# Batch 1's split rows: q's two halves in one product over two PSUM banks, their sums on VectorE at once, the squares' sum on GpSimd

## The chip, the cores and the metric

The kernel runs on one core of one Trainium2 chip. The metric is the device time of that core in microseconds, as the median of several runs. The engines are TensorE (PE; its weight loads are shown apart as PEld), VectorE (DVE), ScalarE (ACT), GpSimd (POOL) and SyncE (SP), which issues most transfers. Each works through its own queue in order and waits on semaphores for the others.

## What is computed

An attention over channels, for two batches of 6016 tokens and 256 channels, followed by a gated layer and a second layer:

```python
def _attn_ref(q, k, v, tau) -> np.ndarray:
    qn = q / (np.linalg.norm(q, axis=1, keepdims=True) + 1e-06)
    kn = k / (np.linalg.norm(k, axis=1, keepdims=True) + 1e-06)
    s = kn.transpose(0, 2, 1) @ qn / tau
    s = s - s.max(-1, keepdims=True)
    a = np.exp(s)
    a /= a.sum(-1, keepdims=True) + 1e-09
    return (v @ a).astype(np.float32)
...
    gate = 1.0 / (1.0 + np.exp(-(x @ w_gate)))
    val = x @ w_val
    return (gate * val @ w_out).astype(np.float32)
...
    h = x @ w_in
    g = h - np.tanh(h)
    return (g @ w_out).astype(np.float32)
```

The scores of a batch are a 256 x 256 matrix, a sum over all its tokens, so no token of batch 1 can go through the layers before all of batch 1's q and k have been multiplied. The layers have 1536 and 2048 hidden channels.

## The kernel before

**Arithmetic.** A float32 value is held as two rounded halves, hi and lo, and a product is made of three: hi with hi, lo with hi, hi with lo. `split` makes the halves: ScalarE copies with rounding (L104), VectorE subtracts (L105).

**Units.** The main loop goes over units. A unit of layer 1 is 512 tokens and 128 hidden channels: 6 products into a gate tile and 6 into a value tile (`ps`, lines L475, L476, L480 of the helpers `prod_h` and `prod_l`), the sigmoid (L515, ScalarE), gate times value (L516, VectorE). A unit of layer 2 is 6 products into one tile `h`, then `s2_a`: on ScalarE two functions of `h` (L539, L540) and two of the result `u` (L541, L543), on VectorE L544 and L546, which read `h`, then L547 and L548. L546 is the last reader of `h`, and it overwrites `u` in place, so it also stands behind ScalarE's L541 and L543. `part_b` splits a unit's result (L575 ScalarE, L576 VectorE) and `part_c` multiplies it, three units later, into the output tiles `y` or `o`. The units of both layers are sorted by a position number, and so stand mixed.

**PSUM.** There are eight banks of 512 float32 columns. Four belong to the accumulators, and four are a ring (`ring`, tag "ring", `bufs=4`): every gate, value and `h` tile and every side product takes a bank of it. A new tile waits on TensorE for the last reader of the tile that had its bank.

**The side work.** From the third token tile on, batch 1's q and k are multiplied beside the layers. The token rows r = 0 to 46 hold 128 tokens each; r = 0 to 3 were multiplied earlier and are only squared here, and r = 4 to 46, 43 rows, are the split rows. A list `side` holds the steps, some of which follow each unit, spread evenly. A split row has three: `side_split` (halves of q and k into `hl`), `side_square` (ScalarE squares the raw row in place, L666), `side_mm`. The last first calls `side_sum`: VectorE adds the squares to `nacc` (L673), and the loads of row r + 2 are issued on SP, which wait for that add. Then `qk_products` (L283 to L285) makes six products of 256 columns into one ring bank. `side_add`, VectorE's add of that bank to the score sum `sacc` (L686), is not issued there but one unit later, ahead of that unit's side steps, through the list `after`. When all rows are done, `nacc` is summed over the partitions by TensorE (`side_norm_mm`).

Of the kernel before, what the change touches and what calls it, by code (L numbers as in the profile page):

```python
# [18 lines left out]
B, S, D = 2, 6016, 256  # L19
# [50 lines left out]
def attn_moe_kernel(  # L70
# [12 lines left out]
    nc = tc.nc  # L83
    ctx.enter_context(tc.manual_schedule())
    mm = nc.tensor.matmul
# [10 lines left out]
    def ring(name):  # L96
        return pp.tile([P, CH], F32, tag="ring", bufs=4, name=name)
# [5 lines left out]
    def split(hi, lo, src, eng=nc.vector):  # L103
        nc.scalar.copy(hi, src)  # L104
        eng.tensor_sub(lo, src, hi.bitcast(F32))  # L105
# [66 lines left out]
    def pump(n):  # L172
        for _ in range(n):
            if stream[0] is not None and next(stream[0], 1) == 1:
                stream[0] = None
# [64 lines left out]
    def fill(g):  # L240

        if g == 0:
            S1.append(bank("o1", "S1"))
        ps = S1[0].rearrange("p (c j) -> p c j", c=2)
        for r in range(filled[0], filled[0] + FILL[g]):
            for c in range(2):
                mm(ps[:, c], fq["k", r][:, c * P : (c + 1) * P], fq["q", r], start=r == 0 and c == 0, stop=r == sum(FILL) - 1, skip_group_check=True)
        filled[0] += FILL[g]
# [28 lines left out]
                w = qk0["k", r0][:, r, c * P : (c + 1) * P]  # L277
                mm(S0[c], w, qk0["q", r0][:, r, :], start=r0 + r == 0, stop=r0 + r == R - 1)  # L278

    def qk_products(ps, qh, ql, kh, kl, first, last):  # L280
        for c in range(2):
            cs = slice(c * P, (c + 1) * P)
            mm(ps[:, c], kh[:, cs], qh, start=first and c == 0, stop=False, skip_group_check=True)  # L283
            mm(ps[:, c], kh[:, cs], ql, start=False, stop=False, skip_group_check=True)
            mm(ps[:, c], kl[:, cs], qh, start=False, stop=last, skip_group_check=True)  # L285

    def refine(rn, s0, n2):
        nc.vector.tensor_mul(rn, rn, n2)
# [70 lines left out]
    def spill():  # L359
        f = full.pop(0)  # L360
        nc.sync.dma_start(wgv_d[f], wgv_t[f].bitcast(F32))
# [66 lines left out]
    ps = ring("spread")  # L428
# [25 lines left out]
    for ic in range(2):  # L454
        cs = slice(ic * P, (ic + 1) * P)
# [63 lines left out]
    def s2_mm(i, m):  # L519
        n = tiles[i][3]  # L520
        h = yhl[i]
        need(f"wi{m // 2}")
        ps = ring(f"h{i}_{m}")
        prod(ps, n, [pair(wi_t[m // 2], (m % 2) * 2 * P + j * P) for j in range(2)], [(h[:, 0, j, :n], h[:, 1, j, :n]) for j in range(2)])
        live[2, i, m] = ps
# [35 lines left out]
    def part_a(u, between=lambda: None):  # L561

        if u[1:] not in live:
            (s1_mm if u[1] == 1 else s2_mm)(*u[2:])
        between()
        (s1_a if u[1] == 1 else s2_a)(*u[2:])
# [42 lines left out]
    def part_c(u):  # L609
        _, kind, i, c = u  # L610
        _, _, pos, n = tiles[i]
        hl = live.pop((kind, i, c))
        last = (K1 if kind == 1 else K2) - 1
        need(f"wo{c // 2}" if kind == 1 else f"wv{c // 2}")
        acc, wt, tag = (yps, wo_t, "y") if kind == 1 else (ops, wv_t, "o")
        if c == 0:
            acc[i] = [bank(f"{tag}{o}", f"{tag}{i}_{o}") for o in range(2)]
        ws = [pair(wt[c // 2], (c % 2) * D + o * P) for o in range(2)]
        if u[1:] == LAST:
            return finish(hl, ws, pos)  # L620
        x = [(hl[:, 0, :n], hl[:, 1, :n])]
        skip = kind == 2 and i == NT - 1
        for o in range(2):
            prod_h(acc[i][o], n, [ws[o]], x, c == 0, skip)
        for o in range(2):
            prod_l(acc[i][o], n, [ws[o]], x, c == last, skip)
        if c == last:
            if kind == 1:
                pool = mp if i % 2 == 0 or (yp is None and i > NYQ) else yq[0] if yp is None else yp
                h = pool.tile([P, 2, 2, NM], F32R, tag="yhl", name=f"yhl{i}")  # L630
                for o in range(2):
                    split(h[:, 0, o, :n], h[:, 1, o, :n], yps[i][o][:, :n])
                yhl[i] = h
            else:
                for o in range(2):
                    t = m2.tile([P, NM], F32, tag="out", bufs=2, name=f"out{i}_{o}")
                    nc.scalar.copy(t[:, :n], ops[i][o][:, :n])
                    nc.sync.dma_start(outT[o * P : (o + 1) * P, pos : pos + n], t[:, :n])


    qp, qctx, q2ctx, q1 = None, ExitStack(), ExitStack(), {}
# [10 lines left out]
    def side_load(r):  # L652
        if r < R:
            raw = qp.tile([P, 2, D], F32, tag="raw", bufs=2, name=f"raw1_{r}")
            for t, src in ((0, q), (1, k)):
                nc.sync.dma_start(raw[:, t, :], token_rows(src, 1)[:, r, :])
            q1["raw", r] = raw

    def side_split(r):
        raw = q1["raw", r]  # L660
        hl = qp.tile([P, 2, 2, D], F32R, tag="hl", name=f"hl1_{r}")
        split(hl[:, 0], hl[:, 1], raw)
        q1["hl", r] = hl

    def side_square(r):
# [2 lines left out]
    def side_sum(r):  # L668
        raw = q1.pop(("raw", r))
        if r == 0:  # L670
            nc.vector.tensor_copy(q1["N"], raw)
        else:
            nc.vector.tensor_add(q1["N"], q1["N"], raw)  # L673
        side_load(r + 2)

    def side_mm(r):
        side_sum(r)
        hl = q1.pop(("hl", r))
        ps = ring(f"qk1_{r}").rearrange("p (c j) -> p c j", c=2)
        qk_products(ps, hl[:, 0, 0, :], hl[:, 1, 0, :], hl[:, 0, 1, :], hl[:, 1, 1, :], True, True)  # L680
        q1["ps", r] = ps
        after.append(r)

    def side_add(r):
        ps = q1.pop(("ps", r))
        nc.vector.tensor_add(q1["S"], q1["S"], ps)  # L686

    def side_norm_mm():
        ps, ones = ring("norm1"), q1["ones"]
# [76 lines left out]
            units.append((max(pos, START2 + DENSE * (i * K2 + m)), 2, i, m))  # L766
    units.sort()
    nside, started, side0 = len(side), 0, None
    qb, qc, after, awq = [], [], [], []

    ahead = [(1, t, K1 - 1) for t in (0, 1, NT - 1)] + [(2, t, K2 - 1) for t in (0, 1, NT - 2)]
    m2 = None
# [1 line left out]
    def step_b():  # L774
        u = qb.pop(0)
        part_b(u)
        qc.append(u)
# [4 lines left out]
    def aw0(f):  # L782
        need(f"wgv{f}_0", f"wgv{f}_1")
        for ic in range(2):
            aw_block(aT0, rs[0], wgv_t[f], ic, aws[0][f], f"aw0_{f}_{ic}")
        pump(2 + sum(owed))
        owed.clear()
# [20 lines left out]
    for u in units:  # L808
        at, kind, i, c = u
        if kind == 1 and i == 0 and c % 2 == 0 and c // 2 + 1 < NW // 2:  # L810
            if c // 2 + 1 < len(FILL):
                fill(c // 2 + 1)
            aw0(c // 2 + 1)
        if kind == 1 and i == 0 and c >= SPILL and full:
            spill()
        if kind == 1 and i == 1 and c == 2:
            t = cst.tile([P, NM], F32, name="s1_out")
            nc.vector.tensor_copy(t, S1[0])
            nc.sync.dma_start(s1_d, t)
        if kind == 2 and c == 0:  # L820
            while i not in yhl:
                if qb:
                    step_b()
                part_c(qc.pop(0))
        if kind == 2 and i == 0 and c == 0:
            pump(1000)
            cctx.close()
            m2 = ctx.enter_context(tc.tile_pool(name="m2", bufs=1, reuse_waits="tile"))
        if qb and len(qc) == LAG - 1 and qc[0][1:] in ahead:
            part_a(u, lambda: part_c(qc.pop(0)))  # L830
        else:
            part_a(u)
        if qb:
            step_b()
        qb.append(u)
        if u[1:] == (2, NT - 1, K2 - 2):
            s2_mm(NT - 1, K2 - 1)
        while len(qb) + len(qc) > LAG:
            part_c(qc.pop(0))
        if kind == 1 and i == 0 and c % 2 and c // 2 + 2 < NW // 2:  # L840
            owed.append(PUMP0)
        else:
            pump(PUMP0 if i == 0 else PUMP1)
        if kind == 1 and i == 0 and c == K1 - 1:
            pump(1000 if cst is None else 0)
        if cst is None and c + 2 >= NW - 2 and stream[0] is None:
            open_w2()
        if kind == 2 and i == NYQ and c == K2 - 1:
            yctx.close()
            side0 = at  # L850
        if side0 is not None:
            if after:
                side_add(after.pop())
            want = min(nside, int((at - side0) * nside / (SIDE_END - side0)) + 1)
            while started < want:
                if side[started] is not None:
                    side[started]()
                started += 1
        if awq:
            side_aw(*awq.pop(0))  # L860
        if kind == 1 and i == TPB - 1 and c % 2 == 1:
            awq += [(c // 2, 0), (c // 2, 1)]
# [46 lines left out]
```

## Time and profile before

| | us |
|---|---|
| median of 3 runs (lowest, highest) | 2305.57 (2305.44, 2306.1) |
| the profiled execution's own time | 2305.91 |
| its span, first to last instruction | 2303.8 |
| TensorE busy | 2297.8 (100%), 10434 products |
| VectorE busy | 1818.0 (79%), 2896 instructions |
| ScalarE busy | 1580.8 (69%), 2884 instructions |
| GpSimd busy | 74.6 (3%), 57 instructions |

TensorE's products are pipelined: one of 512 columns is shown as 0.39 us long, and the next starts 0.23 us after it, so starts are to be read, not lengths. The time of the engines is the union of their instructions. The chain that ended last is the work that set the end, followed back from the last instruction.

### The profile page before, as it was taken

The numbers are of one execution on the slowest core, as the hardware profiler recorded it, in microseconds if no ns is written. First come the engines' busy times: TensorE is split into PE (matmuls) and PEld (weight loads), VectorE is DVE, ScalarE is ACT, GpSimd is POOL, SyncE is SP. The second block draws the span as 40 slices with busy tenths as digits, with TensorE's granted clock in tenths as the row PEclk, the third lists the DMA queues.
The fourth block names the chain that finished last, engine by engine and source line by source line (L and its number), as shares of the span: only waits on it lengthen the run. The fifth ranks groups of instructions, "written<-read, shape, count | busy, mean of one in ns | idle before, by whom it ended". The sixth has DMA issues, their size and how long they took to land.

```text
span 2303.8 us, 28351 instructions
## 1 busy us (share of the span) xinstructions
PE 2297.8 (100%) x10434; PEld 1928.6 (84%) x10434; DVE 1818.0 (79%) x2896; ACT 1580.8 (69%) x2884; POOL 74.6 (3%) x57
## 2 busy tenths in 40 slices
PE   9999999999999999999999999999999999999999
PEld 8888888888888888888899988888888888888887
DVE  6878889888888888877777777777777777786778
ACT  7657777676776677766666666666666667666668
POOL 5000000000000000000000000000000000000006
PEclk9999999999999999999999999999999999999999
DMA  8630001010101101001110000000000000000000
GB/s 333 247 115 1 24 23 33 29 41 19 37 28 33 37 23 38 2 34 35 55 37 17 4 14 19 1 19 10 10 19 2 18 19 1 19 10 10 10 1 19
DMA packets 39786, 83.08 MB, mean 36 GB/s; under 512 B 4192, under 2 KB 18272, under 8 KB 38112
## 3 DMA queue, kind: packets, MB, share of 16 engines
q1 hardware_dynamic: 39216, 80.89, 10.4%
q8 instruction: 81, 1.33, 0.2%
q14 instruction: 57, 0.47, 0.1%
q10 hardware_dynamic: 432, 0.39, 0.1%
HBM read 62.39 MB, written 18.87 MB: 35 GB/s over the span
## 4 chain that ended last, share of the span: by engine, by line
PE 97%; DVE 1%; ACT 1%; issue 0%; POOLq 0%; DVEq 0%; ACTq 0%
PE ps L476 11%; PE ps L475 11%; PE ps L480 11%; PE o L480 7%; PE h L476 7%; PE h L480 7%; PE h L475 7%; PE o L476 7%; PE o L475 7%; PE y L476 5%; PE y L480 5%; PE y L475 5%; PE S0o L278 1%; PE S0y L278 1%; PE qk L285 0%
## 5 line engine op out<-in xcount | busy, mean ns | idle before, releaser
L475 PE MATMUL ps<-vhl,aw 128*128 128x512 f32 (+1 forms) x1152 | 443.5, 385 | 0.2 <-ACT sg L515 0.2
L476 PE MATMUL ps<-vhl,aw 128*128 128x512 f32 (+1 forms) x1152 | 443.6, 385 | 0.0
L544 DVE TENSOR_TENSOR d<-h,d 128x512 f32<-128x512 f32 (+1 forms) x366 | 247.9, 677 | 235.1 <-ACT d L540 235.0
L575 ACT CAST hl<-s 128x512 fp32r<-128x512 f32 (+1 forms) x385 | 234.9, 610 | 273.0 <-DVE s L548 270.0
L539 ACT ACTIVATE u<-h 128x512 f32<-128x512 f32 (+1 forms) x384 | 226.6, 590 | 245.0 <-PE h L480 244.4
L480 PE MATMUL ps<-vhl,aw 128*128 128x512 f32 (+1 forms) x1152 | 349.8, 385 | 0.0
L546 DVE TENSOR_TENSOR u<-h,u 128x512 f32<-128x512 f32 (+1 forms) x360 | 243.2, 676 | 109.3 <-ACT big L543 109.3
L475 PE MATMUL o<-hl,wv 128*128 128x512 f32 (+2 forms) x770 | 295.8, 384 | 0.2 <-ACT hl L575 0.2
L476 PE MATMUL h<-yhl,wi 128*128 128x512 f32 (+1 forms) x768 | 295.7, 385 | 0.0
L476 PE MATMUL o<-hl,wv 128*128 128x512 f32 (+2 forms) x770 | 295.7, 384 | 0.0
L475 PE MATMUL h<-yhl,wi 128*128 128x512 f32 (+1 forms) x768 | 295.6, 385 | 0.0
L548 DVE COPY_PREDICATED s<-big,d 128x512 f32<-128x512 int16 (+1 forms) x366 | 269.8, 737 | 12.9
L541 ACT ACTIVATE s<-u,c_b 128x512 f32<-128x512 f32 (+1 forms) x384 | 275.3, 717 | 2.0 <-DVE hl L576 2.0
L543 ACT ACTIVATE big<-u,c_m 128x512 bf16<-128x512 f32 (+1 forms) x366 | 260.6, 712 | 0.0
L547 DVE SCALAR_TENSOR_TENSOR s<-s,u 128x512 f32<-128x512 f32 (+1 forms) x360 | 244.9, 680 | 12.3
L475 PEld LDWEIGHTS ps<-vhl,aw 128*128 128x128 f32 x1152 | 216.4, 188 | 41.2 <-ACT sg L515 0.7
L476 PEld LDWEIGHTS ps<-vhl,aw 128*128 128x128 f32 x1152 | 216.4, 188 | 40.7
L480 PEld LDWEIGHTS ps<-vhl,aw 128*128 128x128 f32 x1152 | 215.7, 188 | 41.5
L516 DVE TENSOR_TENSOR sg<-ps,sg 128x512 f32<-128x512 f32 (+1 forms) x288 | 194.2, 674 | 69.6 <-PE ps L480 51.3
L576 DVE TENSOR_TENSOR hl<-s,hl 128x512 fp32r<-128x512 f32 (+2 forms) x362 | 241.4, 667 | 0.5 <-ACT hl L575 0.5
L480 PE MATMUL o<-hl,wv 128*128 128x512 f32 (+2 forms) x770 | 234.2, 385 | 0.5 <-POOL hl L576 0.2
L515 ACT ACTIVATE sg<-ps 128x512 f32<-128x512 f32 (+1 forms) x288 | 169.9, 590 | 92.6 <-PE ps L480 88.3
(170 smaller groups left out, 3594.2 us busy)
## 6 DMA issues: line engine op xcount, KB each, us to landing
vraw<-in_vT_dram SPq DMA_DIRECT2D x22, 512.0 KB, 3.7
out_dram<-out SPq DMA_DIRECT2D x43, 256.0 KB, 2.2
raw_wgv<-in_wgv_dram SPq DMA_DIRECT2D x12, 512.0 KB, 4.5
wgv_d<-wgv SPq DMA_DIRECT2D x6, 1024.0 KB, 11.7
wb<-wgv_d SPq DMA_DIRECT2D x6, 1024.0 KB, 4.8
raw<-in_q_dram SPq DMA_DIRECT2D x47, 128.0 KB, 2.1
raw<-in_k_dram SPq DMA_DIRECT2D x47, 128.0 KB, 2.2
rawq<-in_q_dram SPq DMA_DIRECT2D x8, 512.0 KB, 10.4
```

The source lines that it names most:

```text
L475: mm(ps[:, :n], wh, xh, start=first and j == 0, stop=False, skip_group_check=skip)
L476: mm(ps[:, :n], wl, xh, start=False, stop=False, skip_group_check=skip)
L480: mm(ps[:, :n], wh, xl, start=False, stop=last and j == len(wts) - 1, skip_group_check=skip)
L539: nc.scalar.activation(u, H, AF.Square)
L541: nc.scalar.activation(s, u, AF.Square, scale=C_S, bias=c_b[:, 0:1])
L543: nc.scalar.activation(big, u, AF.Relu, bias=c_m[:, 0:1])
L544: nc.vector.tensor_sub(d, H, d)
L546: nc.vector.tensor_mul(w, H, u)
L547: nc.vector.scalar_tensor_tensor(s, s, C_D, w, op0=ALU.add, op1=ALU.mult)
L548: nc.vector.copy_predicated(s, big.bitcast(I16), d)
L575: nc.scalar.copy(hl[:, 0, cs], x[:, cs])
L576: eng.tensor_sub(hl[:, 1, cs], x[:, cs], hl[:, 0, cs].bitcast(F32))
```

## The change

The two halves of q now lie side by side in `hl`, whose order becomes (half, q or k, channels) to (q or k, half, channels). The rounded k of a row is multiplied with both halves of q in one product of 512 columns, for each of k's two blocks of 128 channels; the low half of k is multiplied with the high half of q, as before, into the first 256 columns. Each block has a ring bank of its own, so a row takes two banks and four products instead of one bank and six products. VectorE adds the four halves of the two banks to `sacc`, four adds of 256 columns, right after the products are issued; the later `side_add` and the list `after` are gone. The squares are copied and added on GpSimd instead of VectorE.

```diff
-    def qk_products(ps, qh, ql, kh, kl, first, last):
+    def qk_products(ps, qhl, kh, kl):
         for c in range(2):
             cs = slice(c * P, (c + 1) * P)
-            mm(ps[:, c], kh[:, cs], qh, start=first and c == 0, stop=False, skip_group_check=True)
-            mm(ps[:, c], kh[:, cs], ql, start=False, stop=False, skip_group_check=True)
-            mm(ps[:, c], kl[:, cs], qh, start=False, stop=last, skip_group_check=True)
+            mm(ps[c], kh[:, cs], qhl.rearrange("p h j -> p (h j)"), start=True, stop=False, skip_group_check=True)
+            mm(ps[c][:, :D], kl[:, cs], qhl[:, 0], start=False, stop=True, skip_group_check=True)
...
-        split(hl[:, 0], hl[:, 1], raw)
+        split(hl[:, :, 0], hl[:, :, 1], raw)
...
         if r == 0:
-            nc.vector.tensor_copy(q1["N"], raw)
+            nc.gpsimd.tensor_copy(q1["N"], raw)
         else:
-            nc.vector.tensor_add(q1["N"], q1["N"], raw)
+            nc.gpsimd.tensor_add(q1["N"], q1["N"], raw)
         side_load(r + 2)
 
     def side_mm(r):
         side_sum(r)
         hl = q1.pop(("hl", r))
-        ps = ring(f"qk1_{r}").rearrange("p (c j) -> p c j", c=2)
-        qk_products(ps, hl[:, 0, 0, :], hl[:, 1, 0, :], hl[:, 0, 1, :], hl[:, 1, 1, :], True, True)
-        q1["ps", r] = ps
-        after.append(r)
-
-    def side_add(r):
-        ps = q1.pop(("ps", r))
-        nc.vector.tensor_add(q1["S"], q1["S"], ps)
+        ps = [ring(f"qk1_{r}_{c}") for c in range(2)]
+        qk_products(ps, hl[:, 0], hl[:, 1, 0], hl[:, 1, 1])
+        for c in range(2):
+            for h in range(2):
+                nc.vector.tensor_add(q1["S"][:, c], q1["S"][:, c], ps[c][:, h * D : (h + 1) * D])
...
-            if after:
-                side_add(after.pop())
```

TensorE at the row r = 8, between a unit of layer 2 and one of layer 1, before: the second half of the row's products, then the gate tile `ps4_5_0` and the start of the value tile `ps4_5_1`. In brackets stands the engine whose semaphore an instruction waits for.

```order
L283 MATMUL qk1_8_3961<-hl1_8_3871 128x256
L284 MATMUL qk1_8_3961<-hl1_8_3871 128x256
L285 MATMUL qk1_8_3961<-hl1_8_3871 128x256
L475 MATMUL ps4_5_0_3968<-vhl4_0_3543,aw2_0_518 128x512
L476 MATMUL ps4_5_0_3968<-vhl4_0_3543,aw2_0_518 128x512
L475 MATMUL ps4_5_0_3968<-vhl4_1_3544,aw2_0_518 128x512
L476 MATMUL ps4_5_0_3968<-vhl4_1_3544,aw2_0_518 128x512
L480 MATMUL ps4_5_0_3968<-vhl4_0_3543,aw2_0_518 128x512
L480 MATMUL ps4_5_0_3968<-vhl4_1_3544,aw2_0_518 128x512
L475 MATMUL ps4_5_1_3969<-vhl4_0_3543,aw2_0_518 128x512 [waits DVE_49]
```

The same place now, from the row's first product on (the line numbers behind the change are one or six lower).

```order
L283 MATMUL qk1_8_0_3969<-hl1_8_3879 128x512
L284 MATMUL qk1_8_0_3969<-hl1_8_3879 128x256
L283 MATMUL qk1_8_1_3970<-hl1_8_3879 128x512
L284 MATMUL qk1_8_1_3970<-hl1_8_3879 128x256
L474 MATMUL ps4_5_0_3979<-vhl4_0_3546,aw2_0_518 128x512 [waits DVE_49]
L475 MATMUL ps4_5_0_3979<-vhl4_0_3546,aw2_0_518 128x512
L474 MATMUL ps4_5_0_3979<-vhl4_1_3547,aw2_0_518 128x512
L475 MATMUL ps4_5_0_3979<-vhl4_1_3547,aw2_0_518 128x512
L479 MATMUL ps4_5_0_3979<-vhl4_0_3546,aw2_0_518 128x512
L479 MATMUL ps4_5_0_3979<-vhl4_1_3547,aw2_0_518 128x512
L474 MATMUL ps4_5_1_3980<-vhl4_0_3546,aw2_0_518 128x512 [waits DVE_49]
```

Six products became four, and the banks moved: `ps4_5_0` now has the bank of the tile `h3_3` (before, it had that of a gate tile), and `ps4_5_1` that of `h3_4`, the unit directly ahead of the row (before, that of `h3_3`).

VectorE at the same row, before: the low half of an earlier unit, the square sum, gate times value, another low half, and the score sum.

```order
L576 TENSOR_TENSOR hl2_3_3_3948<-s3_3_3909,hl2_3_3_3948 128x512 [waits PE_49,Activation_49]
L673 TENSOR_TENSOR nacc_2902<-nacc_2902,raw1_8_3730 128x512
L516 TENSOR_TENSOR sg4_5_3982<-ps4_5_1_3969,sg4_5_3982 128x512 [waits PE_49,Activation_49]
L576 TENSOR_TENSOR hl2_3_4_3985<-s3_4_3938,hl2_3_4_3985 128x512 [waits Activation_49]
L686 TENSOR_TENSOR sacc_2901<-sacc_2901,qk1_8_3961 128x512
```

And now:

```order
L575 TENSOR_TENSOR hl2_3_3_3956<-s3_3_3917,hl2_3_3_3956 128x512 [waits PE_49,Activation_49]
L682 TENSOR_TENSOR sacc_2901<-sacc_2901,qk1_8_0_3969 128x256 [waits PE_49]
L682 TENSOR_TENSOR sacc_2901<-sacc_2901,qk1_8_0_3969 128x256 [waits DVE_49]
L682 TENSOR_TENSOR sacc_2901<-sacc_2901,qk1_8_1_3970 128x256 [waits PE_49]
L682 TENSOR_TENSOR sacc_2901<-sacc_2901,qk1_8_1_3970 128x256 [waits DVE_49]
L515 TENSOR_TENSOR sg4_5_3993<-ps4_5_1_3980,sg4_5_3993 128x512 [waits PE_49,Activation_49]
L575 TENSOR_TENSOR hl2_3_4_3996<-s3_4_3946,hl2_3_4_3996 128x512 [waits Activation_49]
```

The four adds of the scores stand where the square sum stood, two of them behind waits for the row's own products, and the later score sum is gone. The square sum stands on GpSimd, which has nothing else to do in this part of the program.

## Rows read from the trace of the kernel before

**Rows 1.** The page: span, busy time by engine, the chain that ended last.

```profile
span 2303.8 us, 28351 instructions
...
PE 2297.8 (100%) x10434; PEld 1928.6 (84%) x10434; DVE 1818.0 (79%) x2896; ACT 1580.8 (69%) x2884; POOL 74.6 (3%) x57
...
PE 97%; DVE 1%; ACT 1%; issue 0%; POOLq 0%; DVEq 0%; ACTq 0%
```

**Rows 2.** The side work's stretch: length, busy us by engine, clock, DMA share, GB/s.

```profile
380.00:940.00 560.00, 560.00 (x2590) 468.21 (x2589) 475.64 (x745) 395.43 (x714) 0.00 (x0) 1.00 0.10 31
```

**Rows 3.** Timeline around r = 8: start, length in us, engine, line, tiles, [idle before].

```profile
426.26 0.39 PE L475 MATMUL h<-yhl,wi 128*128 128x512 f32 x1
...
427.81 0.64 ACT L666 ACTIVATE raw<-raw 128x512 f32<-128x512 f32 x1
...
428.89 0.75 DVE L548 COPY_PREDICATED s<-big,d 128x512 f32<-128x512 int16 x1
428.98 0.28 PE L283 MATMUL qk<-hl 128*128 128x256 f32 x1
...
429.70 0.40 PE L475 MATMUL ps<-vhl,aw 128*128 128x512 f32 x1
...
429.93 0.40 PE L476 MATMUL ps<-vhl,aw 128*128 128x512 f32 x1
...
430.74 0.67 DVE L546 TENSOR_TENSOR u<-h,u 128x512 f32<-128x512 f32 x1
431.08 0.39 PE L475 MATMUL ps<-vhl,aw 128*128 128x512 f32 x1
...
433.40 0.70 DVE L673 TENSOR_TENSOR nacc<-nacc,raw 128x512 f32<-128x512 f32 x1
...
435.20 0.70 DVE L686 TENSOR_TENSOR sacc<-sacc,qk 128x512 f32<-128x512 f32 x1
```

**Rows 4.** Timeline at r = 4, 19 and 46: last `h` reader, first value product.

```profile
383.68 0.69 DVE L546 TENSOR_TENSOR u<-h,u 128x512 f32<-128x512 f32 x1 [0.53 <-ACT big L543]
383.69 0.39 PE L475 MATMUL ps<-vhl,aw 128*128 128x512 f32 x1
...
579.75 0.39 PE L475 MATMUL ps<-vhl,aw 128*128 128x512 f32 x1
...
580.37 0.69 DVE L546 TENSOR_TENSOR u<-h,u 128x512 f32<-128x512 f32 x1 [0.53 <-ACT big L543]
...
937.58 0.68 DVE L546 TENSOR_TENSOR u<-h,u 128x512 f32<-128x512 f32 x1
...
937.92 0.39 PE L475 MATMUL ps<-vhl,aw 128*128 128x512 f32 x1
```

**Rows 5.** Timeline at r = 33: value tile's first product, VectorE's square sum, next.

```profile
769.18 0.39 PE L475 MATMUL ps<-vhl,aw 128*128 128x512 f32 x1
...
769.85 0.70 DVE L673 TENSOR_TENSOR nacc<-nacc,raw 128x512 f32<-128x512 f32 x1
...
770.46 0.70 DVE L544 TENSOR_TENSOR d<-h,d 128x512 f32<-128x512 f32 x1
```

**Rows 6.** Timeline at 75 us, where TensorE waits for a bank.

```profile
74.81 0.58 ACT L515 ACTIVATE sg<-ps 128x512 f32<-128x512 f32 x1
...
75.45 0.50 PE L475 MATMUL ps<-vhl,aw 128*128 128x512 f32 x1 [0.23 <-ACT sg L515]
...
75.78 0.40 PE L476 MATMUL ps<-vhl,aw 128*128 128x512 f32 x1
```

**Rows 7.** Groups by line and form: xcount | busy us, mean ns | idle before.

```profile
L261 POOL TENSOR_TENSOR sumq<-sumq,sqq 128x512 f32<-128x512 f32 x8 | 10.2, 1276 | 3.8 <-ACT sqq L258 1.7 <-DVE sumq L268 1.7
...
L268 DVE TENSOR_TENSOR sumk<-sumk,sqk 128x256 f32<-128x256 f32 x3 | 1.3, 421 | 4.1 <-ACT sqk L266 3.6 <-DVE sumk L268 0.5
```

**Rows 8.** Timeline near the end: GpSimd beside a VectorE instruction.

```profile
2236.82 1.30 POOL L576 TENSOR_TENSOR hl<-s,hl 128x512 fp32r<-128x512 f32 x1 [6.27 <-ACT hl L575]
...
2237.94 0.78 DVE L548 COPY_PREDICATED s<-big,d 128x512 f32<-128x512 int16 x1
```

More of the change, by code (lines that the diff above doesn't have):

```diff
@@ L768, in attn_moe_kernel @@
     nside, started, side0 = len(side), 0, None
-    qb, qc, after, awq = [], [], [], []
+    qb, qc, awq = [], [], []
     ahead = [(1, t, K1 - 1) for t in (0, 1, NT - 1)] + [(2, t, K2 - 1) for t in (0, 1, NT - 2)]
```

## The prediction

> **What bounds the kernel now.** I read the page first: TensorE is busy for all but 6 of its 2303.8 us, and the chain of work that ended last is 97% TensorE [rows 1]. The change lies where batch 1's q and k are multiplied beside the expert layers, so next I read the table by stretches for 380 to 940 us [rows 2]: TensorE 560.00 of 560 us at the full granted clock (1.00, the 2.4 GHz level), VectorE 475.64, ScalarE 395.43, GpSimd nothing. Every TensorE instruction taken away there shortens the run, and every wait that TensorE gains lengthens it by its whole length. VectorE has 84 us to spare, some 2 us for each of the 43 split rows.
>
> Then I read the timeline around one of these rows, r = 8 [rows 3]. The products of a unit of layer 2 (tile `h`) start at 426.26, the six qk products at 428.98, gate tile `ps` of the following layer-1 unit at 429.70, and its value tile at 431.08. The reader is to see how far VectorE is behind: the last reader of that `h`, L546, ends at 430.74 + 0.67 = 431.41, and the row's own square sum (L673) and score sum (L686) come at 433.40 and 435.20, long after the products.
>
> **The change part by part.**
>
> *Products.* Six starts fill 0.72 us, 0.12 each (428.98 to 429.70), a product of 512 columns takes 0.23 (429.70 to 429.93) [rows 3]. Two of 512 and two of 256 make 0.70, so 0.02 to 0.03 us a row, about 1 us over 43 rows. Where TensorE must wait right behind, the gain only lengthens that wait, so I count 0.6 us.
>
> *Banks.* This is the term that decides. The ring has four banks. Before, a row took one; now it takes two. Where a unit of layer 2 stands ahead of the row and one of layer 1 behind it, the sequence is `h`, qk, qk, gate, value: the fifth tile needs the bank of the first, `h`, and the built program does put it there (in r = 8 the value tile sits in the bank of the `h` just ahead; before, it had that of the `h` one unit earlier). The order shows the wait on VectorE at the value tile's first product; what it waits for is now L546 of the unit directly ahead. At r = 8 that ends at 431.41 and TensorE wants to start at 431.08: 0.33 us late.
>
> I made the same subtraction (end of the `h` tile's L546 less the start of the value tile's first product, both in the trace of before, with the banks of the changed program) at all 20 rows that have this order. At 17 of them the bank comes late, first at 383.69 and last at 937.92 [rows 4]: 11 by 0.32 to 0.39 us (sum 3.75), two by 0.69 (2 x 0.69 = 1.38; 383.68 + 0.69 = 384.37 against 383.69), two by 1.05 (2.10), and two by 1.26 and 1.31 (2.57; 580.37 + 0.69 = 581.06 against 579.75). That is 9.80 us. Three have 0.2 us to spare.
>
> Where two layer-2 units stand around the row (6 rows), the later value tile gets the first qk bank. It is free after the first two of the new adds, which stand where L673 stood. At r = 33: 769.85 + 0.84 = 770.69 against 769.18, 1.51 late [rows 5]; two others are 0.78 and 0.51 late, together 2.80 us; three have 0.12 to spare. The other 17 rows have 1 us or more, and two further tiles at r = 33 are late by under 0.1, which I leave to the VectorE term below. Raw sum 12.6 us in 20 places.
>
> *What a wait costs beyond its lateness.* The trace has one such wait at 75.45: ScalarE ends at 74.81 + 0.58 = 75.39, TensorE starts 0.06 later, and its second product follows after 0.33 instead of 0.23 [rows 6]. So 0.06 + 0.10, some 0.16 us each, 20 x 0.16 = 3.2 us.
>
> *Adds on VectorE.* The square sum (0.70) and the score sum (0.70) go [rows 3]; four adds of 256 columns from PSUM come. The trace has that very form, 421 ns [rows 7]: 4 x 0.42 = 1.68. Net 0.3 us a row, 12 us in all, under the 84 us that VectorE idles. They now stand at the earlier of the two places, so VectorE is 1.0 us later (1.68 - 0.70) until the place where L686 stood, and 0.3 later until its next idle gap. In the row of r = 8 they start 3 us after the products end, so they don't wait for TensorE; in a few rows VectorE gets there before they end and idles, which its spare time covers. Queued behind them on VectorE are the value product (L516) and the low half for the output product (L576), on which TensorE waits. That 1.0 us falls on TensorE only where VectorE has no gaps, as around 770 [rows 5], in some eight rows: between 0 and 8 x 1.0 us. I take 1 us, since the waits counted above give VectorE time in several of these rows.
>
> *Squares on GpSimd.* No such add stands in this stretch; the same form at the start takes 1276 ns [rows 7]. It can start when ScalarE's square ends (427.81 + 0.64 = 428.45 at r = 8) and so ends at 429.73, 4 us before VectorE was done with it [rows 3]. The loads of row r + 2 on SP are released earlier, not later, and nothing on SP queues behind them longer. The norm product is over a unit behind the last add. I cost it at nothing as long as it doesn't slow VectorE (below).
>
> *Layout of the halves.* ScalarE and VectorE write the same 512 elements in pieces of 256; no extra instruction. Nothing, within 0.05 us either way.
>
> The sum: 12.6 + 3.2 + 1 - 0.6 = 16.2 us. The profiled execution took 2305.91 us (span 2303.8 and 2.1 around it), the median of runs is 2305.57; the change lies inside the span, so 2321.8 to 2322.1. I forecast **2322**. Its own range: without any restart cost and with 1 us saved, 11.6 (2317); with VectorE's delay felt in most gapless rows, 22 (2328).
>
> **The rivals.**
>
> *GpSimd holds VectorE up.* At r = 8 the GpSimd add would run from 428.45 to 429.73. VectorE's L548, at 428.89, reads two SBUF tiles, and so does L576 behind it. If VectorE can't read two SBUF tiles while GpSimd reads, L548 starts at 429.73, 0.84 later, and L546, three places on, ends 0.84 later too; the value tile waits 1.17 instead of 0.33. In all 17 places that is 14 us on top, 2336; in a third of them 5 us, 2327. It speaks for it that VectorE is busy 85% of the stretch, most of it in such instructions; against it, near the end GpSimd ran from 2236.82 to 2238.12, L548 with its two SBUF inputs started inside that, at 2237.94, and took 0.78 [rows 8] where it took 0.75 at 428.89 [rows 3]: no 0.18 us block is seen. A second pair 10 us later shows none either, but both meet only the tail of the GpSimd instruction.
> The Trainium skill, "SBUF — State Buffer", section "Who interferes with whom", states the rule behind this: a VectorE instruction with two SBUF inputs contends with a GpSimd instruction that reads SBUF, and whichever issued first keeps the shared interface for its whole instruction. By that rule the time is the 2327 to 2336 above; the pair just shown doesn't agree with it, though it is too short an overlap to refute it.
>
> *VectorE runs earlier, and no bank is late: not slower.* VectorE loses two adds of 0.70 a row. If these are what makes L546 late, it ends 0.69 earlier relative to TensorE in every row: the eleven waits of 0.34 and the two of 0.69 vanish, 1.05 becomes 0.36, 1.26 and 1.31 become 0.57 and 0.62; with the qk banks likewise 0.09 and 0.82 are left. That is 2.8 us plus six restarts of 0.16, less 1 us of products: about 2308.7, no change that can be told. The point from which it decides is L546 by 0.34 us. Against it: four adds take the place of the two, 0.3 us a row more, and L546 also waits for ScalarE's pass over the same tile.
>
> *The change doesn't do what it says to TensorE.* If the two PSUM banks made no wait at all, only the products would remain: 1 us less, 2305, and even if a merged product cost its 512 columns at 2.4 GHz alone (0.213 us against 2 x 0.12) no more than 2 x 0.027 x 43 = 2.3 us less. So there is almost no way to a clear gain.
>
> **How the numbers follow.** Bank waits alone 0.56 (2317 to 2328). With GpSimd's clash 0.24 (2327 to 2336). Smaller waits, some of them regained, 0.06 (2311 to 2317). VectorE earlier, or no bank waits, 0.08 (2303 to 2309, of which 0.02 below 2301). Above 2336, VectorE falling behind for good, 0.06. The range 2312 to 2336 leaves out the 0.08, the 0.06 and a little of the small waits. A difference within 0.2% (4.6 us) can't be told from no change here: faster 0.02, same 0.06, slower 0.92.
>
> **What would show it.** In the profile after: about 43 x 2 = 86 fewer products; gaps of 0.5 us on TensorE ahead of value tiles at L474 (L475 of before) that end with VectorE's L545 (L546), about twenty, none inside the qk products; VectorE's busy time up by 12 us, GpSimd's by 47 x 1.28 = 60 us. If the GpSimd clash is real, L546 to L548 and L576 of before get longer or later right after the squares. I am wrong if TensorE's waits before value tiles sum to under 8 us or over 25, or if they end with something else than the `h` bank or the qk adds.

## The result, and the profile after

The changed kernel takes 2330.02 us in the median of 5 runs (2329.88 to 2331.38), the kernel before 2306.07 (2305.44 to 2306.1). The ratio is 1.0105, with a 95% interval of 1.0094 to 1.0116: slower by 24 us. That lies in the range that was forecast, but above the likeliest case's own range (2317 to 2328) and where the GpSimd rival was priced (2327 to 2336). So the wide range held through the rival's part of it, not through the case on which 2322 rests. The profile of after tells which parts were right.

The page of after (span, busy time by engine, chain that ended last), against [rows 1]:

```profile
span 2328.2 us, 28434 instructions
...
PE 2305.8 (99%) x10348; PEld 1921.5 (83%) x10348; DVE 1854.9 (80%) x2978; ACT 1581.7 (68%) x2884; POOL 139.1 (6%) x104
...
PE 87%; DVE 7%; ACT 3%; DMA 1%; issue 1%; SPq 0%; POOLq 0%; DVEq 0%; ACTq 0%
```

The span grew by 24.4 us (2303.8 to 2328.2). TensorE's products fell by 86, as forecast, and GpSimd's time rose by 64.5 us (60 forecast). VectorE's rose by 36.9, where 12 were forecast: the first sign that something besides the four adds is there. In the chain of work that ended last, VectorE now has 7%, where it had 1%.

The stretch of the side work (length, busy us of PE, PEld, DVE, ACT, POOL, then clock, DMA share and GB/s), against [rows 2], which shows TensorE busy without a gap:

```profile
380.00:960.00 580.00, 564.50 (x2493) 459.66 (x2492) 511.36 (x826) 395.16 (x712) 57.63 (x43) 1.00 0.10 30
```

TensorE's waits in 370 to 970 us of after (engine and tile waited for, us in total, times, longest):

```profile
PE ps L474 <- DVE u L545: 13.6, 17, 1.5
PE ps L474 <- DVE sacc L682: 2.1, 2, 1.2
```

Seventeen waits for the last reader of an `h` tile and two for the score adds: the forecast had 17 and 3, and a sum between 8 and 25. The view counts only the time in which the pipeline shows nothing. What the run pays is seen by starts: the pitch from one product to the next, less that of an undisturbed product (0.227 us for 512 columns and 0.120 for 256). So counted, 380 to 945 us holds 23.6 us of lost time, where before had 0.4, and 945 to 1020 us holds 2.4, where before had 0.3. These 25.3 us, less 86 starts that are gone (about 1 us), make up the 24.4 us of the span. Of them 21.0 us lie at the nineteen waits shown, each with the late start of the product behind it. The rest is two short waits for `h` that the view doesn't count (0.6 us together), 1.3 us after the rows (run 2 comes back to them), and gaps of about a tenth and less. So most of the loss is in the forecast places; but many of the waits are longer than the forecast's lateness.

Where the length comes from is seen at r = 8. The timeline of after (start, length, engine, line, tiles, [idle before]), against [rows 3]:

```profile
429.52 0.64 ACT L665 ACTIVATE raw<-raw 128x512 f32<-128x512 f32 x1
...
430.29 1.43 POOL L672 TENSOR_TENSOR nacc<-nacc,raw 128x512 f32<-128x512 f32 x1 [13.27 <-ACT raw L665]
...
430.60 1.74 DVE L547 COPY_PREDICATED s<-big,d 128x512 f32<-128x512 int16 x1
430.69 0.39 PE L283 MATMUL qk<-hl 128*128 128x512 f32 x1
...
431.38 0.40 PE L474 MATMUL ps<-vhl,aw 128*128 128x512 f32 x1
...
432.33 0.62 PE L479 MATMUL ps<-vhl,aw 128*128 128x512 f32 x2
...
433.43 0.67 DVE L545 TENSOR_TENSOR u<-h,u 128x512 f32<-128x512 f32 x1
...
434.16 0.51 PE L474 MATMUL ps<-vhl,aw 128*128 128x512 f32 x1 [1.21 <-DVE u L545]
434.50 0.40 PE L475 MATMUL ps<-vhl,aw 128*128 128x512 f32 x1
```

The four products fill 0.69 us (430.69 to 431.38), as forecast. But the VectorE instruction beside GpSimd's add, L547 (L548 of before, 0.75 us in [rows 3]), takes 1.74. So L545, three places on, ends at 434.10 and TensorE starts the value tile at 434.16, which is 1.38 us after its gate products let it (the last two start from 432.33 on, and 432.33 + 2 x 0.227 = 432.78). The forecast was 0.33 us late plus 0.06. The next product follows after 0.34 instead of 0.23, the forecast restart.

The groups of after by line and form in 380 to 965 us (xcount | busy us, mean ns | idle before):

```profile
L547 DVE COPY_PREDICATED s<-big,d 128x512 f32<-128x512 int16 x92 | 79.7, 866 | 3.1
L546 DVE SCALAR_TENSOR_TENSOR s<-s,u 128x512 f32<-128x512 f32 x92 | 76.2, 829 | 3.1
...
L682 DVE TENSOR_TENSOR sacc<-sacc,qk 128x256 f32<-128x256 f32 x172 | 68.2, 417 | 3.6 <-PE qk L284 0.7
...
L545 DVE TENSOR_TENSOR u<-h,u 128x512 f32<-128x512 f32 x91 | 62.4, 686 | 25.9 <-ACT big L542 25.9
```

The score adds cost what was forecast (417 ns against 421 in [rows 7]). L547 and L546, whose inputs both lie in SBUF, have become longer in the mean, as the first experiment shows beside them. L545, which reads `h` in PSUM and one tile in SBUF, has not.

### The profile page after: what moved, and what is told of

Read it like the earlier page. It is cut to its first block, busy times and chain, and to the rows that moved or that the text cites. A ratio compares the mean times of both kernels' runs of the same rounds, so it can differ in the third digit from the quotient of the medians.

```text
span 2328.2 us, 28434 instructions
## 1 busy us (share of the span) xinstructions
PE 2305.8 (99%) x10348; PEld 1921.5 (83%) x10348; DVE 1854.9 (80%) x2978; ACT 1581.7 (68%) x2884; POOL 139.1 (6%) x104
## 4 chain that ended last, share of the span: by engine, by line
PE 87%; DVE 7%; ACT 3%; DMA 1%; issue 1%; SPq 0%; POOLq 0%; DVEq 0%; ACTq 0%
PE ps L474 10%; PE ps L479 10%; PE ps L475 10%; PE h L475 7%; PE h L474 7%; PE h L479 7%; PE o L479 6%; PE o L474 6%; PE o L475 6%; PE y L474 5%; PE y L475 5%; PE y L479 5%; DMA rawk<-in_k_dram 1%; DVE u L545 1%; DVE hl L575 1%
## 5 line engine op out<-in xcount | busy, mean ns | idle before, releaser
L474 PE MATMUL ps<-vhl,aw 128*128 128x512 f32 (+1 forms) x1152 | 446.8, 388 | 15.9 <-DVE u L545 13.6
L543 DVE TENSOR_TENSOR d<-h,d 128x512 f32<-128x512 f32 (+1 forms) x366 | 247.3, 676 | 224.6 <-ACT d L539 223.2
L545 DVE TENSOR_TENSOR u<-h,u 128x512 f32<-128x512 f32 (+1 forms) x360 | 242.8, 674 | 109.5 <-ACT big L542 109.5
L474 PE MATMUL o<-hl,wv 128*128 128x512 f32 (+2 forms) x770 | 296.0, 385 | 0.2 <-ACT hl L574 0.2
L474 PE MATMUL h<-yhl,wi 128*128 128x512 f32 (+1 forms) x768 | 296.0, 385 | 0.0
L475 PE MATMUL h<-yhl,wi 128*128 128x512 f32 (+1 forms) x768 | 295.8, 385 | 0.0
L547 DVE COPY_PREDICATED s<-big,d 128x512 f32<-128x512 int16 (+1 forms) x366 | 281.6, 769 | 12.9
L474 PEld LDWEIGHTS ps<-vhl,aw 128*128 128x128 f32 x1152 | 216.3, 188 | 67.9 <-DVE u L545 21.8
L546 DVE SCALAR_TENSOR_TENSOR s<-s,u 128x512 f32<-128x512 f32 (+1 forms) x360 | 257.5, 715 | 12.3
L575 DVE TENSOR_TENSOR hl<-s,hl 128x512 fp32r<-128x512 f32 (+2 forms) x362 | 241.8, 668 | 0.5 <-ACT hl L574 0.5
L479 PE MATMUL h<-yhl,wi 128*128 128x512 f32 (+1 forms) x768 | 233.2, 385 | 0.0
```

Of the source, the lines that this page charges most:

```text
L474: mm(ps[:, :n], wh, xh, start=first and j == 0, stop=False, skip_group_check=skip)
L475: mm(ps[:, :n], wl, xh, start=False, stop=False, skip_group_check=skip)
L479: mm(ps[:, :n], wh, xl, start=False, stop=last and j == len(wts) - 1, skip_group_check=skip)
L543: nc.vector.tensor_sub(d, H, d)
L545: nc.vector.tensor_mul(w, H, u)
L546: nc.vector.scalar_tensor_tensor(s, s, C_D, w, op0=ALU.add, op1=ALU.mult)
```

## The experiments

Every kernel below computes the whole function. In the expectations, theory A is both causes together: two banks a row make the last reader of `h` late for TensorE, and GpSimd's add, which reads SBUF, holds VectorE up on top of that. Rival B is the late banks alone, with the longer waits put down to VectorE's four adds. Rival C is GpSimd's add alone. The kernel before took 2305.79 to 2305.96 us beside these runs.

**1. After, with the squares back on VectorE.**

```diff
-            nc.gpsimd.tensor_add(q1["N"], q1["N"], raw)
+            nc.vector.tensor_add(q1["N"], q1["N"], raw)
```

> The changed kernel with the squares' copy and sum back on VectorE; all else as changed. Theory A (late banks, and on top of them VectorE held up by GpSimd's reads of SBUF): TensorE's waits fall from some 23 us to the 13 to 16 us that the subtraction in the trace of before gave, the typical wait from 1.4 to 0.4 us, and the time from 2330 to 2320 to 2324. Rival B (late banks alone; the larger waits come from VectorE's four adds): VectorE has 0.7 us a row more to do, so the time stays or rises, 2329 to 2334. Rival C (GpSimd's reads alone, banks harmless): 2305 to 2308.

It took 2324.97 us, ratio 1.0083 (1.0069 to 1.0096): a microsecond above theory A's range and well below rival B's. The same groups in its trace, then those of before (380 to 940 us):

```profile
L547 DVE COPY_PREDICATED s<-big,d 128x512 f32<-128x512 int16 x92 | 68.9, 749 | 3.1
...
L546 DVE SCALAR_TENSOR_TENSOR s<-s,u 128x512 f32<-128x512 f32 x92 | 63.7, 692 | 3.1
```

```profile
L548 DVE COPY_PREDICATED s<-big,d 128x512 f32<-128x512 int16 x92 | 69.1, 751 | 3.1
L547 DVE SCALAR_TENSOR_TENSOR s<-s,u 128x512 f32<-128x512 f32 x91 | 63.0, 692 | 3.1
```

Without GpSimd's adds the instructions are as short as before. So GpSimd lengthens L547 by 92 x (0.866 - 0.749) = 10.8 us and L546 by 92 x (0.829 - 0.692) = 12.6. That, not the adds, is the greater part of the 25 us by which VectorE's time was under-forecast. TensorE's waits in it, 370 to 970 us:

```profile
PE ps L474 <- DVE u L545: 7.3, 17, 1.2
PE ps L474 <- DVE sacc L682: 4.8, 6, 1.5
```

The same 17 rows, with 7.3 us where after has 13.6. But this kernel keeps the square add on VectorE and has four score adds too, so VectorE is later at other places (six waits for the score adds, not two). It therefore doesn't measure the clash alone; run 5 does.

**2. Before, with only the squares on GpSimd.**

```diff
-            nc.vector.tensor_add(q1["N"], q1["N"], raw)
+            nc.gpsimd.tensor_add(q1["N"], q1["N"], raw)
```

> The kernel before with nothing changed but the squares' copy and sum moved to GpSimd. Theory A: the same VectorE instructions grow longer (two SBUF inputs, 690 to 750 ns each before), but the banks have 1.7 us and more to spare nearly everywhere, so little reaches TensorE: 2305 to 2309. Rival B: VectorE is relieved by 30 us and nothing grows: 2304 to 2306. Rival C: most of the loss is here, 2320 to 2330.

It took 2307.46 us, ratio 1.0008 (0.9999 to 1.0017): no difference that can be told, and in theory A's range. Its timeline at r = 8, and its stretch:

```profile
428.40 1.43 POOL L673 TENSOR_TENSOR nacc<-nacc,raw 128x512 f32<-128x512 f32 x1 [13.39 <-ACT raw L666]
428.71 1.74 DVE L548 COPY_PREDICATED s<-big,d 128x512 f32<-128x512 int16 x1
...
430.90 0.39 PE L475 MATMUL ps<-vhl,aw 128*128 128x512 f32 x1
```

```profile
380.00:960.00 580.00, 579.98 (x2678) 484.48 (x2678) 490.50 (x725) 409.93 (x736) 57.45 (x42) 1.00 0.10 30
```

The stop is there to the last digit, 1.74 us, and TensorE doesn't notice: the value tile starts without a wait, since with one bank a row its bank is that of an older `h`. So the clash by itself costs nothing that can be told; it needs the two banks to reach TensorE.

The 1.6 us by which it lies above before may still be real, since the times of this run (2306.94 to 2308.59) hardly overlap those of before (2305.14 to 2306.97). But the trace loses them behind the rows, not in them: by starts 0.7 us in 380 to 945 us, where before lost 0.4, and 1.6 us in 960 to 1020, where before lost 0.3. Ahead of that, ScalarE loads a table for the square root of the norms. Before, the load ran ahead of VectorE's L293, which prepares the root's input; here it waits for it (before, then this run):

```profile
947.41 1.28 ACT L294 ACT_TABLE_LOAD   x1
```

```profile
949.08 1.28 ACT L294 ACT_TABLE_LOAD   x1 [1.57 <-DVE n L293]
```

The same wait of 1.6 us stands in every kernel here that has the squares on GpSimd, and in none that has them on VectorE. Why the load stands behind it, and whether all of the 1.3 us come from it, isn't shown.

**3. Before, with only the two banks** (the six products kept, two adds of 256 columns at once, squares on VectorE).

```diff
-            mm(ps[:, c], kh[:, cs], qh, start=first and c == 0, stop=False, skip_group_check=True)
+            mm(ps[c][:, :D], kh[:, cs], qh, start=True, stop=False, skip_group_check=True)
...
-        ps = ring(f"qk1_{r}").rearrange("p (c j) -> p c j", c=2)
+        ps = [ring(f"qk1_{r}_{c}") for c in range(2)]
...
-        after.append(r)
+        side_add(r)
```

> The kernel before with its six products of 256 columns, but each of k's two blocks in a ring bank of its own (256 of its 512 columns used), and VectorE's add split in two of 256 columns and issued right behind the products; squares on VectorE. Theory A and rival B: the same value tiles wait for the bank of the unit ahead, 13 to 16 us in 17 to 20 places: 2319 to 2324. Rival C: 2305 to 2308.

It took 2321.92 us, ratio 1.0071 (1.0057 to 1.0085), 16.1 us more than before. Its waits:

```profile
PE ps L475 <- DVE u L546: 7.4, 17, 1.1
PE ps L475 <- DVE sacc L687: 1.9, 2, 1.0
```

Seventeen again. The prediction's bank term with its restarts was 12.6 + 3.2 = 15.8 us; this run measures 16.1.

**4. Before, with only the score add right behind the products.**

```diff
-        after.append(r)
+        side_add(r)
```

> The kernel before with its one bank and six products, but VectorE's score add issued right behind the products instead of one unit later. It is what the run with two banks alone is to be held against. Theory A: a bank is free earlier and nothing else is late: 2305 to 2307. A rival, that it is the place of the adds in VectorE's order that delays TensorE (products, then value product and low half behind an add that waits): 2312 and more.

It took 2306.06 us, ratio 1.0000 (0.9991 to 1.0009), and TensorE has no gap:

```profile
380.00:960.00 580.00, 580.00 (x2680) 484.91 (x2679) 491.27 (x767) 411.10 (x739) 0.00 (x0) 1.00 0.10 30
```

The place of the add is free; in run 3 it is the banks that cost.

**5. After, with GpSimd's add held back until the row's score adds are done** (it first copies one column of the score sum).

```diff
     def side_mm(r):
-        side_sum(r)
...
                 nc.vector.tensor_add(q1["S"][:, c], q1["S"][:, c], ps[c][:, h * D : (h + 1) * D])
+        nc.gpsimd.tensor_copy(q1["tick"], q1["S"][:, 1, D - 1 : D])
+        side_sum(r)
```

> The changed kernel, but GpSimd's add of a row is made to start only when VectorE's four score adds of that row are done (a one-column copy of the score sum on GpSimd stands ahead of it). The same 43 adds hold up VectorE, but some 4 us later, behind the L545 on which the value tile waits. Theory A: VectorE's instructions still grow by some 20 to 27 us in sum, the typical wait of TensorE falls from 1.4 to 0.4 us, and the time comes near that of the run with the squares back on VectorE: 2320 to 2325. A rival, that what VectorE loses to GpSimd is lost wherever it falls: 2328 to 2331.

It took 2322.63 us, ratio 1.0074 (1.0060 to 1.0088). Its waits, and the timeline at r = 8:

```profile
PE ps L474 <- DVE u L545: 8.0, 17, 1.2
PE ps L474 <- DVE sacc L682: 1.8, 2, 1.0
```

```profile
429.43 0.76 DVE L547 COPY_PREDICATED s<-big,d 128x512 f32<-128x512 int16 x1
...
431.15 0.62 PE L479 MATMUL ps<-vhl,aw 128*128 128x512 f32 x2
431.28 0.67 DVE L545 TENSOR_TENSOR u<-h,u 128x512 f32<-128x512 f32 x1
...
432.01 0.50 PE L474 MATMUL ps<-vhl,aw 128*128 128x512 f32 x1 [0.24 <-DVE u L545]
...
435.93 1.29 POOL L673 TENSOR_TENSOR nacc<-nacc,raw 128x512 f32<-128x512 f32 x1
436.11 1.65 DVE L575 TENSOR_TENSOR hl<-s,hl 128x512 fp32r<-128x512 f32 x1
```

The same add now starts 4.0 us after L545 has ended (431.95), so L547 has its 0.76 us and the wait is 0.24 of idle time instead of 1.21 (by starts 432.01 - 431.15 - 2 x 0.227 = 0.41). It still stops a VectorE instruction, L575 (1.65 us for 0.68), but one that TensorE doesn't yet wait for. With everything else of after in place but the loads of row r + 2, which start later together with the add and end no wait of TensorE here, the time is that of the forecast, 2322. The 7.4 us between this run and after (7.1 by each one's difference from its own runs of before) are what the clash costs where it stands ahead of L545.

**6. After, with a row's products put off until the unit just issued is one of layer 1,** squares on VectorE, and the same with the squares on GpSimd.

```diff
             while started < want:
+                if started in held and kind == 2:
+                    break
```

> The changed kernel with the squares back on VectorE, and the row's products held until the unit just issued is one of layer 1 (they are put off by a unit or two where it is one of layer 2). Nothing is left out. The sequence h, qk, qk, gate, value can't come up, so by theory A no bank is late beyond a tenth: 2304 to 2308, as before the change, less up to 1 us for the products. If two banks a row cost something else too (restarts, VectorE's 256-column adds), 2310 to 2320.

> As the run with the rows held back, but with the squares on GpSimd as in the change. Theory A: VectorE's instructions grow by 20 to 27 us in sum as in the change, but now no value tile waits for a bank released at once behind them: 2305 to 2310. If the hold-up reaches TensorE by another way: 2312 and more.

They took 2307.45 us, ratio 1.0008 (0.9999 to 1.0017), and 2309.55, ratio 1.0016 (1.0007 to 1.0025). TensorE's stretch in the first, then the waits of the second:

```profile
380.00:960.00 580.00, 579.15 (x2585) 478.37 (x2584) 524.09 (x895) 408.88 (x736) 0.00 (x0) 1.00 0.10 30
```

```profile
PE qk L283 <- DVE hl L105: 0.6, 1, 0.6
PE ps L474 <- DVE sg L515: 0.3, 2, 0.2
PE o L479 <- DVE hl L575: 0.2, 1, 0.2
```

Both keep the merged products, both banks and the four adds; only the place among the units differs, and no wait for an `h` tile is left. In the second VectorE is stopped as in after (L547 has a mean of 853 ns there), and it is 2.1 us slower than the first. By starts only 0.3 us of that lie in 380 to 945 us, beside the rows; 1.4 lie in 945 to 1020, where the table load waits as in run 2. So it is not two banks as such that cost 16 us, but their place right behind a unit of layer 2.

**7. After, with each of a row's two blocks a step of its own,** squares on VectorE.

```diff
-    def side_mm(r):
-        side_sum(r)
+    def side_mm(r, c):
+        if c == 0:
+            side_sum(r)
...
-            side += [lambda r=r: side_split(r), lambda r=r: side_square(r), lambda r=r: side_mm(r)]
+            side += [lambda r=r: side_split(r), lambda r=r: side_square(r), lambda r=r: side_mm(r, 0), lambda r=r: side_mm(r, 1)]
```

> The changed kernel with the squares back on VectorE, and each row's two blocks (one merged product of 512 columns and one of 256, one ring bank, two adds) issued as two steps of the side work instead of one. Nothing is left out. Only one bank is taken at a time, so by theory A the value tile gets its old spare time of some 2 us: 2304 to 2308. If the merged products or the adds of 256 columns themselves cost time, 2310 to 2320.

A miss: 2326.74 us, ratio 1.0092 (1.0078 to 1.0106). Its waits say why:

```profile
PE qk L282 <- DVE hl L105: 5.7, 7, 1.8
PE ps L473 <- DVE u L544: 4.3, 8, 1.2
PE ps L473 <- DVE sacc L681: 1.5, 3, 0.5
PE ps L473 <- ACT sg L513: 0.6, 1, 0.6
```

(Its lines are one lower than those of after.) The `h` waits are only halved, since the list of steps is spread evenly over the units: with four steps a row instead of three, 15 of the 43 rows still have both blocks in one gap between units, by the order of the program. And seven products now wait for their own row's split (L105), which stands too close ahead of them: by the order of the program in the same gap at one row (r = 42), and one gap ahead at six.

**8. The same, with a block put off to the next gap where this gap has already had the row's split or its other block.**

```diff
             while started < want:
+                if last is not None and started in blocks:
+                    break
```

> The row is four steps as in the run with one block a step, squares on VectorE, but a step that multiplies a block of q and k is put off to the next gap between units when this gap has already taken the row's split or its other block. In the run with one block a step, 15 of the 43 rows still had both blocks in one gap, and 7 products waited for a split of the same gap. Theory (the loss comes only from tiles whose bank's last reader is too near, by where steps fall among the units): both kinds of wait go, TensorE's waits in 380 to 960 us sum to under 3 us, and the time is 2306 to 2311. Rival (a row in four steps crowds VectorE, whatever gap they fall in): waits on VectorE stay, 2318 to 2327.

It took 2319.95 us, ratio 1.0061 (1.0044 to 1.0077): outside the theory's range and in the rival's. Its waits, and the timeline at one of them:

```profile
PE qk L282 <- DVE hl L105: 6.5, 7, 1.7
PE ps L473 <- ACT sg L513: 1.4, 2, 0.7
PE ps L473 <- DVE sacc L681: 0.5, 1, 0.5
```

```profile
526.51 0.63 ACT L104 CAST hl<-raw 128x512 fp32r<-128x512 f32 x1
...
527.59 0.73 DVE L546 COPY_PREDICATED s<-big,d 128x512 f32<-128x512 int16 x1
...
528.22 0.67 DVE L574 TENSOR_TENSOR hl<-sg,hl 128x512 fp32r<-128x512 f32 x1
...
528.82 0.68 DVE L105 TENSOR_TENSOR hl<-raw,hl 128x512 fp32r<-128x512 f32 x1
...
529.55 0.50 PE L282 MATMUL qk<-hl 128*128 128x512 f32 x1 [1.70 <-DVE hl L105]
```

All eight waits on `h` are gone and 6.8 us with them, which is what the theory of the banks says. Seven waits on the split stay, against it. The expectation took all seven waiting rows of run 7 to have their split in the same gap; only r = 42 had, so the edit left the other six as near as they were. In this run all seven stand one gap behind their split. That is too little, since the split's subtraction stands behind VectorE's own queue (ScalarE is done at 527.14, L105 begins at 528.82). The rival, that four steps crowd VectorE in whatever gap, is not refuted. So here the price of more steps is a wait of another kind. Some 3 us more are lost after the rows, in 960 to 1020 us, where the steps that finish the scores also stand closer together; I didn't pursue these.

## Why the prediction came out as it did

**The bank term was right, in places and size.** 17 waits for `h` were forecast, and 17 came, all ahead of value tiles at L474, at the same 17 rows in after and in runs 1, 3 and 5. Run 3 alone gives 16.1 us for the forecast 15.8, and it fits place by place: by starts eleven waits are 0.39 or 0.40 us, two 0.75 and 0.76, two 1.11 and one 1.32, each the forecast's lateness plus about 0.06. Only r = 19 is off (0.79 where 1.31 + 0.06 were forecast). At r = 8 run 5 has its value tile 0.41 us late by starts; the forecast was 0.33 + 0.06. Of the three score-add waits two came, with 2.1 us.

**Products and adds** were forecast at -0.6 and +1 us. Run 5, which has them and the squares off VectorE, is 0.8 us slower beside before than run 3 (16.8 against 16.1, each to its own runs of before): right, within what can be told. Run 5 also has the later table load, 1.3 us more than run 3 in 945 to 1020 us, which no term of the forecast has. Run 1 suggests that the sign depends on the square add: with it still on VectorE, the merged products and the four adds cost 3 us (19.1 against 16.1).

**The squares "at nothing" was the step that failed.** The forecast's condition was that GpSimd doesn't slow VectorE, and it does: the 7.4 us between run 5 and after are the missing term, and with it the sum of 16.2 becomes 23.6, near the measured 24. It is so large because of what it meets. Going by starts, place by place, nine of the waits are longer in after than in run 5: five by 0.96 to 0.98 us and four by 0.35 to 0.39, together 6.3; eight of them are waits for `h` and one is for a score add. Two waits for `h` that run 5 doesn't have, at r = 17 and 38, add 0.6: they are among the three rows for which the forecast had 0.2 us to spare. How the stop is lost at the other places I didn't follow.

**Why I set the rival low: a pair read wrongly.** I took [rows 8] as evidence against a block of 0.18 us, since L548 started at 2237.94, before GpSimd's end at 2238.12, and was only 0.03 longer. But the start shown is that of the issue, and a stopped instruction is shown as a longer one. Counting back its own 0.75 from its end at r = 8 of after (430.60 + 1.74 = 432.34) puts its work from 431.59 on, while GpSimd's end is shown at 431.72: it lets go some 0.13 us before its shown end (0.12 to 0.15 in the 30 such pairs of after). By that, L548 in [rows 8] could begin at about 2237.99 and had only 0.05 us to lose. The row agreed with the rule to within some 0.02 us. I had even noted that the pair met only the tail; that should have left the rival near the full weight of the rule, not at 0.24.

The rule itself stands in the Trainium skill, "SBUF — State Buffer", section "Who interferes with whom": a VectorE instruction with two SBUF inputs contends with a GpSimd instruction that reads SBUF, the one that issued first keeps the shared port, and a VectorE instruction with at most one SBUF input, outside its two-port modes, doesn't contend. The runs agree on each point. L546 and L547 get longer by up to 1.0 us. At r = 8, where L546 began ahead of GpSimd's add, it is the add that is longer (1.43 us for 1.29 in run 5). And the readers of `h`, with one input in PSUM, are not stopped: L543 began inside a GpSimd add eight times in after and took 692 ns in the mean, against 687 elsewhere; L545 did so nine times in run 5, with 685 against 689.

**The rival's own price** was 14 us where all 17 places are hit and 5 where a third are. Eight of the 17 were hit, five of them in full, and the score add of one more row: 7.4. Its picture at r = 8 (0.84 us later) was right in kind; the stop was 0.99, since GpSimd began 0.13 us after ScalarE's square, not at once, and its add was longer by about as much as it lets go ahead of its end.

## What to carry to other kernels

A wait's price depends on how far the reader that frees a buffer is behind the engine that wants it: count the distance in buffers between the two for every order of the neighbours, as here for 20 rows, and the sum comes out. An instruction moved to an idle engine isn't free where it stops those of the busy one, as GpSimd's add does here; whether that costs anything is decided by what waits for the stopped instruction, so two edits that cost 0 to 2 and 16 us alone cost 24 together. Before a short overlap in a trace is taken as evidence against such a clash, compute how much the rule would have lengthened that very pair.

## What the runs showed that was not expected

- A GpSimd add of 128 x 512 float32 stops VectorE instructions with two SBUF inputs for about 1.0 us each at most (1.74 for 0.75, 1.65 for 0.68), and all of it is shown as busy time of VectorE: 866 and 829 ns in the mean instead of 749 and 692. So a busy share that rises is not always more work.
- GpSimd's add also becomes longer where VectorE came first: 1.43 us at r = 8 against 1.29 in run 5.
- 24 us of extra span came with the full granted clock (1.00) in every stretch shown, before and after: none of it is clock.
